# Two small reorderings in a Fourier-mixing and SwiGLU kernel: where the squares of a norm stand on ScalarE, and where the second filter product stands on VectorE

## The chip, the cores and the metric

The kernel runs on one core of one Trainium2 chip. Its time is the device time of one execution in microseconds (us). Before the change the median of three runs is 863.48 us (862.96 to 863.52). A profile of one execution is at hand as well; its own clock runs from the first to the last instruction.

A core has engines with a queue each: TensorE (PE in the profile, with its weight loads listed as PEld), VectorE (DVE), ScalarE (ACT), GpSimd (POOL) and SyncE (SP), which here only starts transfers. Each works through its own queue in order and waits there for semaphores of the others. TensorE writes its products into PSUM, which is cut into banks; VectorE and ScalarE read them out.

## The reference

The input x has 8 batches of 3008 positions with 256 features. Along the positions each feature is taken to its spectrum, multiplied by a complex filter, and brought back:

```python
X = np.fft.rfft(x, axis=1)
Y = X * (filt_r + 1j * filt_i)[None, :, :]
y = np.fft.irfft(Y, n=x.shape[1], axis=1)
```

The 24064 rows of y then go through a root-mean-square norm and a gated feed-forward of inner width 1536:

```python
xn = x / np.sqrt(np.mean(x * x, axis=-1, keepdims=True) + 1e-06) * rms_g
g = xn @ w_gate
out = (g * (1.0 / (1.0 + np.exp(-g))) * (xn @ w_val)) @ w_out
```

## The kernel before

The Fourier transform of length 3008 = 47 x 64 is done as products with small matrices, batch by batch, in four stages. The first stage (`a_unit`, line 201) is one product per unit, tile `psa`, 12 units per batch, read out to `t` and stored to memory. The middle stage (`b_unit`, line 236) takes four small products into one bank, tile `psb`, 16 units per batch. Its read-out is at the same time the product with the filter: two VectorE instructions, one with the real part (`s_part` with e = 0, line 231) and one with the imaginary part (e = 1, line 234). Both read the same bank, so the bank is free when the second is through. GpSimd adds the two (`add_unit`, line 268), and SyncE transposes the sum (`yt_load`, line 275). In batch 1 every fourth unit is a `b_soft` (line 247), which ScalarE copies out for GpSimd to work on. The third stage (`bi_unit`, line 280) multiplies back, tile `psi`, read out by ScalarE to `uu` (line 195). The last stage (`n_unit`, line 306) gives the rows of y, tile `psn`, read out by ScalarE. ScalarE then squares and sums these rows (`sq_unit`, line 322, one instruction for each 256 columns, so mostly two in a unit), GpSimd makes the scale from the sums (`stat_unit`, lines 330 and 332) and applies it (`xt_unit`), and SyncE transposes the scaled rows to `xn` (`tr_unit`).

The feed-forward is the bulk. It is cut into 576 slots: 8 batches, 6 groups of up to 512 rows, 12 blocks of 128 inner columns. In slot i, `gv` (line 533) makes four products of 512 columns on TensorE: two into `pg` (gate), two into `pv` (value). ScalarE then makes `sg` from `pg` (line 550), and VectorE multiplies `pv` by `sg` to `hh` (line 551). Two slots later `down` (line 554) multiplies `hh` with the output weights into `po`. Both `pg` and `pv` have two banks each, so the `pv` products of slot i+2 need `hh` of slot i to be through. The end of each group of 12 slots copies `po` out, half on ScalarE (line 568) and half on VectorE (line 569).

The Fourier stages of batch b+1 run between the feed-forward slots of earlier batches. They use two PSUM banks of one buffer each, called 0 (pool `psM`) and 3 (pool `psB`) in `bank` (line 189). A unit in bank 0 or 3 can begin its products only when the unit before it in that bank has been read out.

The order of the instructions is written out by hand: a planner (`fit`, line 734) gives every unit a slot from costs of ScalarE and VectorE and from when a bank is taken, and the list `plan[i]` holds the units of slot i. In that list the functions of `front` (line 720: squares, second filter product, add) stand ahead of the others, and so they also stand ahead in the engines' queues. The loop from line 837 emits, for every slot i, first `gv(i)`, then the units of `plan[i]`, then `down` of the item two slots back. So on VectorE a second filter product planned for slot i comes behind `hh` of slot i, and on ScalarE the order in a slot is `sg`, squares, read-outs. One exception stands in lines 832 to 834: where the next slot has an `a_unit` in bank 0 and this slot has a `bi_unit`, the squares go to the end of the list.

```python
            for fn, a in plan.pop(i, ()):
                fn(*a)
```

Of the kernel before, what the change touches and what calls it, by code (L numbers as in the profile page):

```python
# [101 lines left out]
def kernel(  # L102
# [430 lines left out]
    def gv(b, m, jt):  # L533
        n = nq(b, m)
        xn = st[b]["xn"][m]
        parts = ((0, 2), (2, 4)) if (b, m, jt) in SPLIT else ((0, n),)
        sg = hp.tile([P, 512], FP16, tag="sg", name="sg")
        hh = hhs[(6 * JT * b + JT * m + jt) % 4]
        made = []
        for q0, q1 in parts:  # L540
            w = (q1 - q0) * P
            pg = psG.tile([P, 512], FP32, tag="pg", name="pg")
            pv = psV.tile([P, 512], FP32, tag="pv", name="pv")
            for ps, wt in ((pg, wg), (pv, wv)):
                for dt_ in range(2):
                    nc.tensor.matmul(ps[:, 0:w], wt[:, dt_, ts(jt, P)], xn[:, q0:q1, dt_, :],  # L546
                                     start=(dt_ == 0), stop=(dt_ == 1))
            made.append((pg, pv, w, slice(q0 * P, q1 * P)))
        for pg, pv, w, c in made:
            nc.scalar.activation(out=sg[:, c], in_=pg[:, 0:w], func=AXT.Silu)  # L550
            nc.vector.tensor_tensor(out=hh[:, c], in0=pv[:, 0:w], in1=sg[:, c], op=ALU.mult)  # L551
        hh_of[(b, m, jt)] = hh

    def down(b, m, jt):
        hh = hh_of.pop((b, m, jt))
        if jt == 0:
            po_of[(b, m)] = [psO.tile([P, 2, D], FP32, tag="po%d" % i, name="po%d" % i)
                             for i in range(2)]
        po = po_of[(b, m)]

        n = nq(b, m)
        for s4 in range(n):
            nc.tensor.matmul(po[s4 // 2][:, s4 % 2, :], hh[:, ts(s4, P)], wo[:, jt, :],  # L563
                             start=(jt == 0 and s4 % 2 == 0),
                             stop=(jt == JT - 1 and (s4 % 2 == 1 or s4 == n - 1)))
        if jt == JT - 1:
            o3 = op.tile([P, 4, D], FP32, tag="o3", name="o3")
            nc.scalar.activation(out=o3[:, 0:2, :], in_=po[0], func=AXT.Copy)
            nc.vector.tensor_copy(out=o3[:, 2:n, :], in_=po[1][:, 0:n - 2, :])
            po_of[(b, m)] = o3  # L570

    def o_store(b, m):
        o3 = po_of.pop((b, m))
        w = 3 if m == 5 else 4
        if b == B - 1 and m == 5:
            row = lambda q, n: raw(out, b * N + 4 * m + q, [[N1 * D, N2], [H * D, 2], [1, n * D]])
            nc.sync.dma_start(row(0, 2), o3[:, 0:2, :].rearrange("p q d -> p (q d)"))
            nc.sync.dma_start(row(2, 1), o3[:, 2, :])
            nc.scalar.dma_start(raw(out, b * N + H - 1, [[N1 * D, N2], [-N * D, 2], [1, D]]), o3[:, 3, :])
            return  # L580
        nc.sync.dma_start(raw(out, b * N + 4 * m, [[N1 * D, N2], [H * D, 2], [1, w * D]]),
                          o3[:, 0:w, :].rearrange("p q d -> p (q d)"))
        if m == 5 and b % 2:
            nc.sync.dma_start(raw(out, b * N + H - 1, [[N1 * D, N2], [-N * D, 2], [1, D]]), o3[:, 3, :])
# [25 lines left out]
    with tc.manual_schedule():  # L610
# [108 lines left out]
        plan, late = {}, {}  # L719
# [109 lines left out]
            for m in range(6):  # L829
                norm_plan(b, m, (n_at + 8 * m, n_at + 8 * m + (4 if b > 1 else 2)), (2, 3, 7) if b > 1 else (2, 3, 6))  # L830

        for i, now in plan.items():
            if any(fn == a_unit and a[3] == 0 for fn, a in plan.get(i + 1, ())) and bi_unit in [fn for fn, _ in now]:
                now.sort(key=lambda u: u[0] == sq_unit)

        stores = {}
        for i in range(len(items) + 4):
            if i < len(items):
                gv(*items[i])
            for fn, a in plan.pop(i, ()):  # L840
                fn(*a)
            if 2 <= i < len(items) + 2:
                b, m, jt = items[i - 2]
                if jt == 1 and i > JT:
                    down(b, m, 0)
                if jt or i < JT:
                    down(b, m, jt)
                if items[i - 2][2] == JT - 1:
                    stores[i + 1] = items[i - 2][:2]
            for fn, a in late.pop(i, ()):  # L850
                fn(*a)
            if i in stores:
                o_store(*stores[i])
        assert not plan and not late


# [28 lines left out]
```

## Time and profile before

| | |
|---|---|
| median of the three runs | 863.48 us |
| profiled execution, first to last instruction (span) | 861.4 us |
| median less span | 2.1 us |
| TensorE busy | 852.4 us (99%) |
| VectorE busy | 557.2 us (65%) |
| ScalarE busy | 612.4 us (71%) |
| GpSimd busy | 297.8 us (35%) |
| granted TensorE clock | 0.999 of full speed |
| first feed-forward product | 43.4 us |
| last matmul | 856.3 us |

The profiled execution gives its span only; what lies around the span in a timed run is put at the 2.1 us between the two. The timeline lists instructions by engine in order of time: start, duration, engine, line, operation, written tile, read tiles, shapes; equal neighbours are drawn together with their number. A matmul's row begins where its product starts to flow; its successor starts while the row still lasts, so two rows of one engine overlap. The waits table lists, by engine, whom idle time before an instruction is put down to.

### The profile page before, as it was taken

The page shows a single profiled execution, that of the slowest core. Times are in us where ns is not written, and L with a number is a line of the kernel's source. Part 1 is how long each engine was busy: PE and PEld are TensorE (multiplying, and loading weights), DVE is VectorE, ACT ScalarE, POOL GpSimd, SP SyncE. Part 2 cuts the span into 40 slices and gives each one's busy share as a digit, 9 for nine tenths or more (in the row PEclk, how much of TensorE's full clock was granted, in tenths as well). Part 3 has the DMA queues.
Part 4 walks back from the last instruction along what each step waited for, and adds up shares of the span by engine and source line. Part 5 has one row for each costly group of instructions (what it writes and reads, how often), then busy time and mean ns, then how long its engine had stood idle before and what let it go on. Part 6 is the DMA issues. An engine that isn't in the chain of part 4 may idle for free.

```text
span 861.4 us, 17024 instructions
## 1 busy us (share of the span) xinstructions
PE 852.4 (99%) x6142; PEld 532.2 (62%) x6142; DVE 557.2 (65%) x926; ACT 612.4 (71%) x1339; POOL 297.8 (35%) x346
## 2 busy tenths in 40 slices
PE   8999999999999999999999999999999999999997
PEld 6755666566666666666666666666666666665664
DVE  5857655776666666666666676767666665555554
ACT  4986777787588756887577856888567765777443
POOL 5725742453144322534034430444123430132000
PEclk9999999999999999999999999999999999999999
DMA  9995778765975476656755548433564331521101
GB/s 283 270 204 124 150 164 168 139 130 121 197 137 129 121 150 111 151 107 147 139 127 113 132 98 180 108 87 101 131 127 93 97 70 42 124 54 49 62 25 50
DMA packets 198237, 107.98 MB, mean 125 GB/s; under 512 B 158566, under 2 KB 182520, under 8 KB 198152
## 3 DMA queue, kind: packets, MB, share of 16 engines
q1 hardware_dynamic: 189464, 85.52, 44.1%
q0 software_dynamic: 8544, 21.24, 12.7%
q8 instruction: 48, 0.79, 0.4%
q14 instruction: 37, 0.30, 0.1%
q10 hardware_dynamic: 144, 0.13, 0.0%
HBM read 45.78 MB, written 35.65 MB: 95 GB/s over the span
## 4 chain that ended last, share of the span: by engine, by line
PE 96%; DMA 1%; ACT 1%; DVE 1%; issue 0%; POOL 0%; POOLq 0%
PE po L563 28%; PE pg L546 28%; PE pv L546 28%; PE psb L241 3%; PE psi L285 3%; PE psn L314 2%; PE psa L206 2%; DMA fs<-in_filt_i_dram 1%; PE psy L418 1%; PE psf L389 1%; PE pst L367 0%; ACT sg L550 0%; POOL xc L186 0%; DVE s L231 0%; DVE hh L551 0%
## 5 line engine op out<-in xcount | busy, mean ns | idle before, releaser
L551 DVE TENSOR_TENSOR hh<-pv,sg 128x512 f16<-128x512 f32 (+2 forms) x578 | 391.5, 678 | 286.4 <-ACT sg L550 221.9
L550 ACT ACTIVATE sg<-pg 128x512 f16<-128x512 f32 (+2 forms) x578 | 337.4, 584 | 217.6 <-PE pg L546 213.4
L546 PE MATMUL pg<-xn,wg 128*128 128x512 f16 (+2 forms) x1156 | 338.1, 374 | 0.1
L546 PE MATMUL pv<-xn,wv 128*128 128x512 f16 (+2 forms) x1156 | 338.1, 374 | 0.0
L563 PE MATMUL po<-wo,hh 128*128 128x256 f16 x2256 | 332.7, 273 | 0.0
L563 PEld LDWEIGHTS <-hh 128*128 128x128 f16 x2256 | 213.4, 98 | 105.5 <-issue 0.6
L268 POOL TENSOR_TENSOR ss<-s,s 128x384 f16<-128x384 f16 x112 | 101.9, 911 | 273.2 <-DVE s L234 245.2
L546 PEld LDWEIGHTS <-wv 128*128 128x128 f16 x1156 | 112.9, 98 | 130.7
L546 PEld LDWEIGHTS <-wg 128*128 128x128 f16 x1156 | 111.4, 98 | 17.0 <-issue 0.3
L340 POOL TENSOR_TENSOR xt<-y,rho 128x1024 f16<-128x1024 f32 (+1 forms) x46 | 85.4, 1856 | 2.8
L322 ACT ACTIVATE junk<-y 128x256 f16<-128x256 f32 x180 | 74.3, 413 | 2.8
L231 DVE TENSOR_TENSOR s<-psb,ff 128x384 f16<-128x384 f32 x124 | 67.6, 547 | 0.7 <-ACT ff L195 0.6
L234 DVE TENSOR_TENSOR s<-psb,ff 128x384 f16<-128x384 f32 x124 | 67.6, 546 | 0.0
L195 ACT ACTIVATE uu<-psi 128x384 f16<-128x384 f32 (+1 forms) x127 | 61.6, 486 | 1.5 <-DMA out_dram<-o 0.5
L195 ACT ACTIVATE y<-psn 128x512 f32<-128x512 f32 (+1 forms) x95 | 55.7, 588 | 4.2
L285 PEld LDWEIGHTS <-yt 96*128 96x128 f16 x512 | 35.4, 97 | 26.7 <-issue 1.0
L332 POOL TENSOR_TENSOR rho<-u,mhalf 128x4 f32<-128x4 f32 (+1 forms) x46 | 46.5, 1010 | 3.8
L330 POOL TENSOR_SCALAR u<-ss 128x4 f32<-128x4 f32 (+1 forms) x46 | 8.9, 193 | 104.8 <-ACT junk L322 103.8
L195 ACT ACTIVATE t<-psa 128x512 f16<-128x512 f32 x70 | 41.4, 594 | 3.1 <-PE psa L206 1.7
L285 PE MATMUL psi<-wi,yt 96*128 96x96 f16 x512 | 42.9, 205 | 0.1
L241 PE MATMUL psb<-wb,t 96*128 96x96 f16 x480 | 40.1, 206 | 0.3 <-DVE s L234 0.2
L241 PEld LDWEIGHTS <-t 96*128 96x128 f16 x480 | 28.7, 97 | 12.8 <-DVE s L234 3.3
(101 smaller groups left out, 366.2 us busy)
## 6 DMA issues: line engine op xcount, KB each, us to landing
out_dram<-o SPq DMA_DIRECT2D x40, 512.0 KB, 3.6
xc<-in_x_dram POOLq DMA_DIRECT2D x31, 384.0 KB, 5.6
z_tmp<-t SPq DMA_DIRECT2D x28, 384.0 KB, 2.7
t<-z_tmp SPq DMA_DIRECT2D x28, 384.0 KB, 6.0
out_dram<-o SPq DMA_DIRECT2D x7, 384.0 KB, 2.7
fs<-in_filt_i_dram POOLq DMA_DIRECT2D x3, 512.0 KB, 10.8
fs<-in_filt_r_dram POOLq DMA_DIRECT2D x3, 512.0 KB, 11.2
ws<-in_moe_w_gate_dram POOLq DMA_DIRECT2D x3, 512.0 KB, 9.8
```

The lines of the kernel that those rows point to most:

```text
L195: nc.scalar.activation(out=out, in_=in_, func=AXT.Copy, **({} if scale is None else {"scale": scale}))
L231: eng.tensor_tensor(out=o, in0=ps, in1=f1, op=ALU.mult)
L234: eng.tensor_tensor(out=o, in0=ps[:, :, ::-1, :], in1=f2, op=ALU.mult)
L241: nc.tensor.matmul(ps[:, ts(k, KR)], st[b]["t2"][kk // KC][:, kk % KC, ds(dh * P, P)], wb[0:KR, kk, :], start=True, stop=True)
L268: nc.gpsimd.tensor_tensor(out=ss3[g % 3][:, :, dh, 0:KR], in0=s[0], in1=s[1], op=ALU.add)
L285: nc.tensor.matmul(ps[:, k, :], yt[0:KR, k, dh, :], wi[0:KR, 4 * g + k, :], start=True, stop=True)
L322: nc.scalar.activation(out=junk, in_=y[:, i, ts(u, D)], func=AXT.Square, accum_out=ss[:, 2 * i + u:2 * i + u + 1])
L340: nc.gpsimd.tensor_tensor(out=xt[:, 0:n, :], in0=y.rearrange("p a (u d) -> p (a u) d", u=2)[:, 0:n, :], in1=rho[:, 0:n].unsqueeze(2).to_br ...
L546: nc.tensor.matmul(ps[:, 0:w], wt[:, dt_, ts(jt, P)], xn[:, q0:q1, dt_, :], start=(dt_ == 0), stop=(dt_ == 1))
L550: nc.scalar.activation(out=sg[:, c], in_=pg[:, 0:w], func=AXT.Silu)
L551: nc.vector.tensor_tensor(out=hh[:, c], in0=pv[:, 0:w], in1=sg[:, c], op=ALU.mult)
L563: nc.tensor.matmul(po[s4 // 2][:, s4 % 2, :], hh[:, ts(s4, P)], wo[:, jt, :], start=(jt == 0 and s4 % 2 == 0), stop=(jt == JT - 1 and (s4 ...
```

## The change

A helper lists which PSUM banks the units of a slot use. With it two things are decided for every slot i, after the planner is done.

First, squares: where slot i has a read-out by ScalarE (a `bi_unit`, an `n_unit`, or an `a_unit` that ScalarE reads out) and slot i+1 uses bank 0, the squares go behind the other units of slot i. Before, this held only for a `bi_unit` ahead of an `a_unit` in bank 0.

Second, the second filter product: where slot i-1 has a `b_unit` whose bank slot i+1 uses, its second filter product is taken out of `plan[i]` and emitted at the start of slot i, ahead of `gv(i)`. On VectorE it so comes ahead of `hh(i)` instead of behind it.

```diff
-        for i, now in plan.items():
-            if any(fn == a_unit and a[3] == 0 for fn, a in plan.get(i + 1, ())) and bi_unit in [fn for fn, _ in now]:
+        def banks(i):
+            for fn, a in plan.get(i, ()):
+                if fn in (n_unit, bi_unit):
+                    yield 0
+                elif fn == a_unit:
+                    yield a[3]
+                elif fn == b_unit:
+                    yield a[2]
+                elif fn == b_soft:
+                    yield 3
+
+        early = {}
+        for i in sorted(plan):
+            now = plan[i]
+            after = set(banks(i + 1))
+            if any(fn in (bi_unit, n_unit) or (fn == a_unit and a[2] == "A") for fn, a in now) and 0 in after:
                 now.sort(key=lambda u: u[0] == sq_unit)
+            for fn, a in plan.get(i - 1, ()):
+                if fn == b_unit and a[2] in after:
+                    early[i] = [u for u in now if u == (s_part, (a[0], a[1], 1))]
+                    plan[i] = now = [u for u in now if u not in early[i]]
 
         stores = {}
         for i in range(len(items) + 4):
+            for fn, a in early.pop(i, ()):
+                fn(*a)
             if i < len(items):
                 gv(*items[i])
             for fn, a in plan.pop(i, ()):
...
-        assert not plan and not late
+        assert not plan and not late and not early
```

The planner's slots are the same before and after. Worked through the plan, the squares change place in slots 32, 34, 43, 45, 92 and 100, and the second filter product in 21 slots: 20, 22, 25, 27, 29, 31, 37, 39, 41 and 44 in batch 1, and 76, 78, 83, 85, 87, 90, 92, 97, 99, 104 and 106 in batch 2. From batch 3 on nothing moves. The queues of TensorE, GpSimd and SyncE keep their order throughout.

## The prediction

> **What bounds the kernel now.** The page first: TensorE is the chain that ended last.
>
> ```profile
> span 861.4 us, 17024 instructions
> PE 852.4 (99%) x6142; PEld 532.2 (62%) x6142; DVE 557.2 (65%) x926; ACT 612.4 (71%) x1339; POOL 297.8 (35%) x346
> PE 96%; DMA 1%; ACT 1%; DVE 1%; issue 0%; POOL 0%; POOLq 0%
> ```
>
> The reader sees that only time taken out of TensorE's queue can shorten the run; VectorE and ScalarE are idle a third of the span. Next the waits, from 60 to 210 us, where all moved instructions lie. TensorE's own:
>
> ```profile
> PEld L241 <- DVE s L234: 3.3, 7, 0.7
> PE psb L241 <- DVE s L234: 0.2, 1, 0.2
> ```
>
> The weight loads of the middle stage stood 3.3 us behind the second filter product, but a load that waits may still be hidden by running products, and idle time of TensorE itself is put at 0.2 us. From 210 us on the same view names no wait of TensorE at all. So I went to the timeline and read starts, not ends. In undisturbed slots a pair of 512-column products is followed 0.43 us later by the next product, a single one by 0.22, four 256-column ones by 0.43, four 96-column ones by 0.17. What a start comes later than that is a stall. Around 82 us:
>
> ```profile
> 81.43 0.55 DVE L231 TENSOR_TENSOR s<-psb,ff 128x384 f16<-128x384 f32 x1
> 81.89 0.68 DVE L551 TENSOR_TENSOR hh<-pv,sg 128x512 f16<-128x512 f32 x1
> 82.24 0.60 PE L546 MATMUL pv<-xn,wv 128*128 128x512 f16 x2
> 82.49 0.54 DVE L234 TENSOR_TENSOR s<-psb,ff 128x384 f16<-128x384 f32 x1
> 82.95 0.68 DVE L569 COPY o<-po 128x512 f32<-128x512 f32 x1
> 83.09 0.34 PE L241 MATMUL psb<-wb,t 96*128 96x96 f16 x4 [0.25 <-DVE s L234]
> 83.27 0.60 PE L546 MATMUL pg<-xn,wg 128*128 128x512 f16 x2
> 83.70 0.59 PE L546 MATMUL pv<-xn,wv 128*128 128x512 f16 x2
> 84.13 1.04 PE L563 MATMUL po<-wo,hh 128*128 128x256 f16 x8
> ```
>
> `pv` at 83.70 is followed by `po` at 84.13, as it should be. `pv` at 82.24 should be followed by `psb` at 82.67, but that started at 83.09, some 0.06 behind the end of the second filter product (82.49 + 0.54 = 83.03): a stall of 0.41. The filter product stood behind `hh`. The same on ScalarE at 93 us:
>
> ```profile
> 92.14 0.60 ACT L550 ACTIVATE sg<-pg 128x512 f16<-128x512 f32 x1 [0.21 <-PE pg L546]
> 92.37 0.34 PE L285 MATMUL psi<-wi,yt 96*128 96x96 f16 x4
> 92.63 0.41 ACT L322 ACTIVATE junk<-y 128x256 f16<-128x256 f32 x1
> 93.16 0.42 ACT L322 ACTIVATE junk<-y 128x256 f16<-128x256 f32 x1
> 93.58 0.47 ACT L195 ACTIVATE uu<-psi 128x384 f16<-128x384 f32 x1
> 93.58 0.60 PE L546 MATMUL pv<-xn,wv 128*128 128x512 f16 x2
> 93.95 0.59 ACT L550 ACTIVATE sg<-pg 128x512 f16<-128x512 f32 x1
> 94.10 0.38 PE L314 MATMUL psn<-t,tab 128*128 128x512 f16 x1
> ```
>
> `psi` is done by about 92.7, its read-out `uu` runs at 93.58 behind two squares, and `psn`, which wants the bank, starts at 94.10 instead of 94.01, 0.05 behind the end of `uu`.
>
> **The change part by part.** *Second filter product ahead of `hh`, 21 places.* No instruction is added. Its releaser, the first filter product, ends before `hh` in each of these slots, and the two run back to back with 0.46 us from start to start, so the bank comes free some 0.6 us earlier (slot 25: 81.89 + 0.54 = 82.43 instead of 83.03) or more where VectorE had idled before `hh`. With the 0.06 of release to start, slot 26's `psb` could begin at 82.49; it is due at 82.67, so its stall goes whole. Eleven of the 21 places have a stall in the next slot, each 0.05 to 0.15 us behind the end of that filter product: the product starts at 75.16 (0.09 us stalled), 78.25 (0.10), 83.09 (0.41), 89.21 (0.18), 113.48 (0.10), 156.06 (0.09), 159.15 (0.09), 166.84 (0.18), 169.91 (0.09), 188.85 (0.09) and 202.98 (0.09). Unrounded starts sum to 1.54 us. The ten other places have none; there nothing is won.
>
> *Squares behind the read-out, 6 places.* The read-out moves ahead by two squares, 93.58 - 92.63 = 0.95 us, less the time that `psi` is not done. Five stalls end 0.05 us behind such a read-out: `psn` at 94.10 (0.09), `psi` at 97.34 (0.26), `psn` at 111.80 (0.09), `psn` at 181.14 (0.26) and 193.80 (0.09). Unrounded 0.77 us. All are shorter than 0.95 less 0.11 (below), so all go. The sixth place, slot 45, has no stall behind it.
>
> *What it costs on VectorE.* `hh` must now wait for the second filter product: it starts at the earliest 2 x 0.46 us behind the start of the first. From the idle time before `hh` in the 21 slots (0 in three, at 81.89, 84.61 and 103.75; 0.11 to 0.32 in four; 0.37 or more in fourteen) that makes it 0.46 us late in three, at most 0.27 elsewhere, 2.0 us over all. Behind `hh` in VectorE's queue stand the next slot's `hh` or the copy of `po`; but these come no later than before, as the two instructions only change place. The one that waits for the late `hh` is `pv` two slots on: it started 1.13 us (slots 25 and 85) to 2.04 us behind the end of `hh`. The worst case is slot 25: 1.13 - 0.46 - 0.41 of stall gone leaves 0.26, against a release of 0.06. `po` in slot 27 wants its bank, which the copy `o` frees at 83.65 as before; its third product is due at 84.13 + 0.22 - 0.41 = 83.94: 0.29 to spare. So I cost the late `hh` at nothing; without that cover it would be up to 2.0 us once through.
>
> *What it costs on ScalarE.* The read-out may now wait for `psi` with the squares and the next `sg` behind it. Elsewhere `uu` starts 0.37 us behind `psi` (402.33 after 401.96), so at 92.74 instead of 92.63: 0.11 us idle, 0.7 over six places. It falls to the next `sg`, whose `pg` bank is wanted 1.51 us or more after it, and to `hh` behind it, whose `pv` bank has 1.22 us or more. Cost nothing.
>
> *GpSimd and the transfers.* Adds start up to 1 us earlier. In slots 34 and 45 the scale waits for the later squares, and adds queue behind it, by 0.5 us; transposed sums landed 4.0 to 7.0 us and `xn` 3.6 us or more before their first use. SyncE's queue has the same order. Nothing.
>
> *Sum.* 1.54 + 0.77 = 2.31 us off TensorE's queue, in a stretch (75 to 203 us) behind which it never waited, so the end moves as much: span 861.38 - 2.31 = 859.07. The median stands 2.1 us above the span; with that unchanged, 863.48 - 2.31 = 861.17, say 861.2 us (0.27% faster).
>
> *Against the idle rows.* By TensorE's idle time the two changes could win no more than 0.25 us (the one gap in brackets above), and the time would be 863.2. The Trainium skill, Perfetto Trace Analysis, section Tensor Engine Instruction (MATMUL, LD_WEIGHTS), says that a matmul's end in the profile is computed from its size, not observed, and so would have stalls hide inside "busy"; the starts above agree, and by it the sum stays with the starts.
>
> **The rivals.** *The stalls are none:* 99% busy is right, late starts are caught up in the products. Then 863.2. Against it: no product after a late start comes closer than the usual spacing (83.09, 83.27, 83.70, 84.13).
>
> *The wait moves.* VectorE has no idle time from 80.96 to 85.75, and its work there is not less; if half of the 2.31 us comes back at other banks, 862.3. For it: three `hh` late by 0.46. Against: 0.26 us is left at the tightest.
>
> *ScalarE held at its head:* the 0.11 us per place passes to TensorE through `sg`, 0.7 us, so 861.9. The same page of the Trainium skill, same section, calls ScalarE's queue strictly first in, first out, which speaks for such a loss; that the squares held up `uu` here agrees. Against it the 1.22 us above.
>
> *Slower:* the late `hh` reaches `pv` two slots on, at each of the 21 places, with the full 0.46 us: 9.7 us, less 2.3, so 870.9. It decides from where `hh` comes over 1.07 us late (1.13 less 0.06), and slower by over 0.2% needs 4.0 us of it. For it: VectorE's stretch without idle time. Against: idle time of 0.3 us or more before most `hh`.
>
> **How the numbers follow.** Forecast 0.72, no stalls 0.06, wait moves 0.08, ScalarE's head 0.06, slower 0.08. About 0.2% (1.73 us, so 861.75) is what a measurement of this kernel can tell from no change. Faster is the forecast alone, 0.72; the three middle cases give 0.20 within the bound; slower 0.08. The forecast's own range is 860.9 (a few small stalls more) to 861.7. To hold 8 in 10 the range takes in ScalarE's head and the moved wait, with 0.3 us for the spread of the runs (0.56): 860.8 to 862.6.
>
> **What would show it.** In the profile after: `psb` 0.43 us behind the `pv` pair at the eleven places, `psn` and `psi` likewise at five, the waits of weight loads on line 234 gone, from 210 us on the same times less 2.3 us. `hh` starts 0.46 us behind the second filter product at slots 25, 27, 39. Wrong it would be by a new gap before `pv` or `po` two slots after a moved product, or before a `pg` behind moved squares, or by stalls that stay where the bank is free.

## The result, and the profile after

The changed kernel takes 861.05 us in the median of 11 runs (860.79 to 862.05), the kernel before 863.23 us in 11 runs beside it (862.96 to 863.52). The ratio is 0.9976 with a 95% interval of 0.9968 to 0.9985: 2.18 us faster. 861.2 was predicted, in a range of 860.8 to 862.6.

The lines of the changed kernel's page that answer to those of before (of pages, waits and timelines only the rows that the text speaks of are shown here):

```profile
span 859.3 us, 17024 instructions
PE 849.6 (99%) x6142; PEld 532.8 (62%) x6142; DVE 557.2 (65%) x926; ACT 612.7 (71%) x1339; POOL 298.1 (35%) x346
PE 97%; DMA 1%; ACT 1%; DVE 0%; POOL 0%; issue 0%; POOLq 0%
```

The span is 2.1 us shorter, with nearly the same busy time on VectorE and ScalarE. TensorE shows 99% before and after: the share of busy time tells nothing of what changed. In the waits from 60 to 210 us the weight loads of the middle stage, 3.3 us behind the second filter product before, are down to these, the only two rows of TensorE that are left:

```profile
PEld L241 <- issue: 0.2, 1, 0.2
PEld L241 <- DVE s L234: 0.2, 1, 0.2
```

The second is the load at 82.54, and its product, in the timeline below, starts on time: a load can wait at no cost. The first is the load at 79.94 in slot 24, and there, as shown further down, a product does start late, though the view names no engine.

The timeline around slot 25, with the second filter product (line 234) now ahead of `hh`:

```profile
81.48 0.55 DVE L231 TENSOR_TENSOR s<-psb,ff 128x384 f16<-128x384 f32 x1
81.94 0.55 DVE L234 TENSOR_TENSOR s<-psb,ff 128x384 f16<-128x384 f32 x1
82.27 0.59 PE L546 MATMUL pv<-xn,wv 128*128 128x512 f16 x2
82.41 0.68 DVE L551 TENSOR_TENSOR hh<-pv,sg 128x512 f16<-128x512 f32 x1
82.70 0.34 PE L241 MATMUL psb<-wb,t 96*128 96x96 f16 x4
83.00 0.68 DVE L569 COPY o<-po 128x512 f32<-128x512 f32 x1
83.31 0.59 PE L546 MATMUL pv<-xn,wv 128*128 128x512 f16 x2
83.74 1.04 PE L563 MATMUL po<-wo,hh 128*128 128x256 f16 x8
```

`psb` starts 0.43 us behind the `pv` pair, where it was 0.85. `hh` starts 0.47 behind the second filter product, and ends at 83.09, 0.22 us before the `pv` of slot 27 at 83.31. The place on ScalarE, slot 32:

```profile
91.56 0.60 ACT L550 ACTIVATE sg<-pg 128x512 f16<-128x512 f32 x1 [0.21 <-PE pg L546]
91.80 0.34 PE L285 MATMUL psi<-wi,yt 96*128 96x96 f16 x4
92.17 0.49 ACT L195 ACTIVATE uu<-psi 128x384 f16<-128x384 f32 x1
92.55 0.41 ACT L322 ACTIVATE junk<-y 128x256 f16<-128x256 f32 x1
93.01 0.59 PE L546 MATMUL pv<-xn,wv 128*128 128x512 f16 x2
93.08 0.42 ACT L322 ACTIVATE junk<-y 128x256 f16<-128x256 f32 x1
93.44 0.38 PE L314 MATMUL psn<-t,tab 128*128 128x512 f16 x1
```

`uu` ends at 92.66, and `psn` follows its `pv` pair in 0.43 us. But a late start that was not there before has come, in slot 24:

```profile
78.47 0.41 ACT L322 ACTIVATE junk<-y 128x256 f16<-128x256 f32 x1
79.00 0.42 ACT L322 ACTIVATE junk<-y 128x256 f16<-128x256 f32 x1
79.41 0.47 ACT L257 ACTIVATE y<-psb 128x384 f32<-128x384 f32 x1
79.42 0.59 PE L546 MATMUL pv<-xn,wv 128*128 128x512 f16 x2
79.94 0.33 PE L241 MATMUL psb<-wb,t 96*128 96x96 f16 x4
```

`psb` is due at 79.85 and starts at 79.94, 0.06 behind the end of `y`, the copy of a `b_soft` in the same bank. That copy stands behind two squares, and the change moves squares only for other kinds of read-out. Before, TensorE had lost 0.19 us in two stalls ahead of this place, came later by that, and met a free bank.

All starts that come over 25 ns later than the usual spacing, from the first feed-forward product on, sum to 2.81 us before and 0.60 after: 2.21 us. From 60 to 210 us the gaps that no row of TensorE covers are only 0.47 us before (149.53 of 150 us busy) and none after (150.00), so most of the time won had stood inside rows that count as busy. The first feed-forward product started at 43.38 us before and at 43.53 after; in the profiles of this study that start lies between 43.29 and 43.68 whatever the edit.

### The profile page after: what moved, and what is told of

Same layout as the page of the kernel before. It is cut to its first block, busy times and chain, and to the rows that moved or that the text cites. A ratio compares the mean times of both kernels' runs of the same rounds, so it can differ in the third digit from the quotient of the medians.

```text
span 859.3 us, 17024 instructions
## 1 busy us (share of the span) xinstructions
PE 849.6 (99%) x6142; PEld 532.8 (62%) x6142; DVE 557.2 (65%) x926; ACT 612.7 (71%) x1339; POOL 298.1 (35%) x346
## 4 chain that ended last, share of the span: by engine, by line
PE 97%; DMA 1%; ACT 1%; DVE 0%; POOL 0%; issue 0%; POOLq 0%
PE po L563 29%; PE pv L546 28%; PE pg L546 28%; PE psb L241 3%; PE psi L285 3%; PE psn L314 2%; PE psa L206 2%; DMA fs<-in_filt_i_dram 1%; PE psy L418 1%; PE psf L389 1%; PE pst L367 0%; POOL xc L186 0%; DVE s L231 0%; ACT ff L195 0%; ACT L470 0%
```

## The experiments

The theory: products on TensorE start late where their bank is freed late, nothing catches such a start up, and the late starts add up to the difference in time. The rivals: the waits only move; the late `hh` costs; ScalarE is held by a read-out that waits. In this table "late starts" is that sum from the one trace of each kernel, and the last column is against the kernel before in the same comparison. The edits below are shown without the lines around them; they are made to the changed kernel, except where the text says otherwise.

| kernel | late starts, us | less those of before | median, us | median less before |
|---|---|---|---|---|
| before | 2.81 | | 863.22 to 863.26 | |
| changed | 0.60 | -2.21 | 861.05 | -2.18 |
| second filter product alone | 1.36 | -1.45 | 861.69 | -1.53 |
| squares alone | 2.25 | -0.56 | 862.67 | -0.55 |
| squares, and the filter product of slot 44 | 1.95 | -0.86 | 862.41 | -0.85 |
| filter product ahead everywhere | 0.59 | -2.22 | 861.12 | -2.10 |
| before, without the old exception | 5.61 | +2.80 | 865.93 | +2.71 |
| squares behind `b_soft` too | 0.53 | -2.28 | 860.93 | -2.33 |
| squares behind `b_soft`, and those of two more slots moved | 0.94 | -1.87 | 861.35 | -1.91 |

### One half alone: the second filter product

```diff
-            if any(fn in (bi_unit, n_unit) or (fn == a_unit and a[2] == "A") for fn, a in now) and 0 in after:
+            if any(fn == a_unit and a[3] == 0 for fn, a in plan.get(i + 1, ())) and bi_unit in [fn for fn, _ in now]:
```

> Only the second filter product goes ahead of hh (21 places); the squares stay as before. Theory (the stalls at single banks add up along TensorE's queue): the eleven stalls of 1.54 us go, the new one of 0.09 us in slot 24 appears as in the changed kernel, the five stalls behind squares (0.77 us) stay; 1.45 us faster than before, 0.17%. Rival (the wait moves: what is freed at one bank is lost at another unless squares move too): less than 0.8 us faster. Rival (the late hh costs, and the gain comes from the squares): no faster, or slower.

Measured: 861.69 us (861.46 to 862.09), ratio 0.9982 (0.9973 to 0.9991), 1.53 us faster. In the trace all eleven stalls are gone, the one of slot 24 is there (0.09), and the five behind squares stand at 0.09, 0.26, 0.09, 0.26 and 0.09 as before. This half works without the other. The rival by which it costs, and the one by which the freed time is lost elsewhere, fall.

### The other half alone: the squares

```diff
-                if fn == b_unit and a[2] in after:
+                if fn == b_unit and a[2] in ():
```

> Only the squares go behind the read-out (6 places); the second filter product stays behind hh. Theory: the five stalls of together 0.77 us go and the eleven of 1.54 us stay; 0.8 us faster than before, 0.09%, and with the other half alone the two sum to the whole change (2.2 us). Rival (ScalarE held at its head by a read-out that waits for psi): 0.1 us faster or nothing.

Measured: 862.67 us (862.57 to 863.0), ratio 0.9994 (0.9985 to 1.0003): 0.55 us faster where 0.8 was expected. The interval includes no change at all, though the runs of the kernel before lie higher, at 862.97 to 863.5; what follows rests on the trace. The five stalls are gone and ten of the eleven are unchanged to 5 ns. The eleventh, `psa` in slot 45, has grown from 0.10 to 0.31. The timeline of this kernel there:

```profile
109.49 0.60 ACT L550 ACTIVATE sg<-pg 128x512 f16<-128x512 f32 x1
109.72 0.34 PE L285 MATMUL psi<-wi,yt 96*128 96x96 f16 x4
110.10 0.49 ACT L195 ACTIVATE uu<-psi 128x384 f16<-128x384 f32 x1
111.43 0.58 ACT L550 ACTIVATE sg<-pg 128x512 f16<-128x512 f32 x1
112.04 0.69 DVE L551 TENSOR_TENSOR hh<-pv,sg 128x512 f16<-128x512 f32 x1 [0.76 <-ACT sg L550]
112.65 0.55 DVE L234 TENSOR_TENSOR s<-psb,ff 128x384 f16<-128x384 f32 x1
113.25 0.39 PE L206 MATMUL psa<-xc,tab 128*128 128x512 f16 x1
```

From `sg` to `sg` it is 111.43 - 109.49 = 1.94 us here; in the kernel before it was 1.82, as these two rows of its timeline show:

```profile
109.83 0.60 ACT L550 ACTIVATE sg<-pg 128x512 f16<-128x512 f32 x1
111.65 0.59 ACT L550 ACTIVATE sg<-pg 128x512 f16<-128x512 f32 x1
```

`uu` waits for `psi` 0.11 us, the squares and `sg` behind it start as much later, then `hh`, then the filter product behind `hh`, and `psa` waits for that. The other 0.09 of the growth is what TensorE had won in slot 44, and waits away here. So ScalarE held at its head did reach TensorE, at one place of six.

### The squares and one filter product

```diff
-                if fn == b_unit and a[2] in after:
+                if fn == b_unit and a[2] in after and i == 44:
```

> The squares behind the read-out, and the second filter product ahead of hh in slot 44 alone. With the squares alone the stall of psa in slot 45 grew from 0.10 to 0.31 us. Theory: the read-out in slot 43 holds ScalarE's queue for 0.11 us, which passes by sg and hh of slot 44 to the filter product behind hh, and 0.09 us won ahead of it is lost there too; with the filter product ahead of hh that stall goes whole: 0.77 + 0.10 = 0.87 us faster than before, 0.3 us faster than the squares alone. Rival (something else in slot 45 is late): as the squares alone, 0.55 us faster than before.

Measured: 862.41 us (862.23 to 862.99), ratio 0.9991 (0.9982 to 1.0): 0.85 us faster, and no late start in slot 45 in the trace. With the filter product ahead of `hh` the chain from `uu` to `psa` is cut at `hh`. So in the whole change the reordering on VectorE covers a cost of the reordering on ScalarE: by the traces the two halves alone win 1.45 and 0.56, 2.01 us together, and the whole change 2.21.

### The late `hh`, in all places

```diff
-                if fn == b_unit and a[2] in after:
+                if fn == b_unit:
```

> The changed kernel, with the second filter product ahead of hh in all 108 places instead of 21. In the 87 further places no bank is wanted in the next slot, so nothing is to be won there; hh comes later by 0 to 0.47 us, 7.4 us over all. Theory (the late hh is covered by the time until pv two slots on, 0.38 us or more after the shift): the same as the changed kernel within 0.1 us, 2.2 us faster than before. Rival (the late hh reaches TensorE): slower than the changed kernel by up to 7.4 us.

Measured: 861.12 us (860.93 to 861.23), ratio 0.9975 (0.9965 to 0.9985); the changed kernel ran at 861.05 and again at 861.07. `hh` starts later, counted from its own slot's first product, in 29 of the 87 further places, by up to 0.46 us and 7.3 us over all. The late starts on TensorE sum to 0.59 us as in the changed kernel. Of 7.3 us of lateness on VectorE nothing arrives. In these places at least 0.39 us was left between the end of `hh` and `pv` two slots on. TensorE's only wait from 60 us to the end is this one, the load of slot 24 again:

```profile
PEld L241 <- issue: 0.2, 1, 0.2
```

### More of the same cost: squares ahead in 14 more slots

This edit is made to the kernel before.

```diff
-        for i, now in plan.items():
-            if any(fn == a_unit and a[3] == 0 for fn, a in plan.get(i + 1, ())) and bi_unit in [fn for fn, _ in now]:
-                now.sort(key=lambda u: u[0] == sq_unit)
```

> The kernel before, with its old exception for squares taken out too: in 14 slots of batches 3 and 4 the squares stand ahead of the psi read-out where the next slot's psa wants the bank. Theory: the read-out ends 1.91 us after the start of that slot's sg, and psa starts 0.05 us later; against the starts of before this is a stall of 0.26 us in seven slots (136 to 172), 0.51 in two (210, 214) and 0.09 in five (202, 222 to 238): 3.25 us slower than before, 0.38%. Rival (such late starts are caught up and cost nothing at the end): no slower. Rival (the stall is only moved): less than 1.6 us slower.

Measured: 865.93 us (865.62 to 866.2), ratio 1.0031 (1.0019 to 1.0042): 2.71 us slower where 3.25 was expected. Slot 136 of this kernel and the `psa` behind it:

```profile
244.93 0.60 ACT L550 ACTIVATE sg<-pg 128x512 f16<-128x512 f32 x1 [0.88 <-PE pg L546]
245.42 0.41 ACT L322 ACTIVATE junk<-y 128x256 f16<-128x256 f32 x1
245.95 0.42 ACT L322 ACTIVATE junk<-y 128x256 f16<-128x256 f32 x1
246.20 0.59 PE L546 MATMUL pv<-xn,wv 128*128 128x512 f16 x2
246.37 0.47 ACT L195 ACTIVATE uu<-psi 128x384 f16<-128x384 f32 x1
246.89 0.38 PE L206 MATMUL psa<-xc,tab 128*128 128x512 f16 x1
```

`psa` is due at 246.63 and starts at 246.89: the stall of 0.26 that was worked out, and six of the seven slots have it to 2 ns, as five others have their 0.09. Slot 172 has none: one square stands ahead of its read-out there, not two. Slots 210 and 214 have 0.41 instead of 0.51: their `sg` has 384 columns, and the 1.91 us that were expected from its start to the end of the read-out hold for one of 512; here it is 1.81. Thirteen stalls, 2.78 us, make the 2.71.

### Two attempts at a version that beats both

```diff
+            if b_soft in [fn for fn, _ in now] and 3 in after:
+                now.sort(key=lambda u: u[0] == sq_unit)
```

> The changed kernel, with the squares of slot 23 behind the read-out of the b_soft there, whose bank slot 24 uses. Theory: the stall of 0.09 us that the change left in slot 24 goes. But the read-out waits 0.1 us for its product, sg and hh of slot 24 come that much later, and with them hh of slot 25, where pv two slots on had 0.23 us left; 0.23 - 0.11 - 0.09 leaves 0.03, under the 0.05 of a release, so up to 0.03 us may return there: 0.05 to 0.09 us faster than the changed kernel. Rival (0.03 us is no edge, more comes back): the same or slower than the changed kernel.

Measured: 860.93 us (860.78 to 861.13), ratio 0.9973 (0.9962 to 0.9984); beside it the changed kernel itself, whose expectation was

> The changed kernel once more, beside the next three on the same chip: 861.05 us, 2.2 us faster than before.

and which came to 861.07 us (860.86 to 861.13), 0.9974 (0.9964 to 0.9984). The stall in slot 24 is gone. A part came back, not at `pv` as expected but at `psb` in slot 26:

```profile
82.06 0.55 DVE L234 TENSOR_TENSOR s<-psb,ff 128x384 f16<-128x384 f32 x1
82.20 0.59 PE L546 MATMUL pv<-xn,wv 128*128 128x512 f16 x2
82.67 0.34 PE L241 MATMUL psb<-wb,t 96*128 96x96 f16 x4
```

`psb` starts 0.47 us behind the pair, 0.04 late. The lateness went there from `sg` of slot 24 (79.92, in the changed kernel 79.78) by its `hh` (80.53 and 80.40) and VectorE's queue to this filter product (82.06 and 81.94). By the traces 0.07 us is won; by the medians 0.14, with ranges that overlap. This is the fastest kernel of the study, by an amount that these runs don't resolve.

The second attempt adds to this:

```diff
+        for i in (352, 356):
+            sq = [u for u in plan[i] if u[0] == sq_unit]
+            plan[i] = [u for u in plan[i] if u[0] != sq_unit]
+            up_ = [u for u in plan[i + 1] if u[0] == a_unit]
+            plan[i + 1] = up_ + sq + [u for u in plan[i + 1] if u[0] != a_unit]
```

> As the run before, and the squares of slots 352 and 356 one slot later, behind the read-out of psa, for which psi of slots 354 and 358 were 0.05 us late each. Theory: 0.09 us more, so 0.14 to 0.18 us faster than the changed kernel, about 860.9 us. Rival: nothing is gained, since so small a stall is caught up.

Measured: 861.35 us (861.1 to 861.51), ratio 0.9977 (0.9968 to 0.9986): 0.42 us slower than the run before. The expectation fell. The two late starts of `psi` are gone, but the squares now stand ahead of the next `sg` and the read-out of `psi` (slot 354):

```profile
552.37 0.41 ACT L322 ACTIVATE junk<-y 128x256 f16<-128x256 f32 x1
552.65 0.34 PE L285 MATMUL psi<-wi,yt 96*128 96x96 f16 x4
552.90 0.42 ACT L322 ACTIVATE junk<-y 128x256 f16<-128x256 f32 x1
553.32 0.47 ACT L550 ACTIVATE sg<-pg 128x384 f16<-128x384 f32 x1
553.65 0.49 PE L546 MATMUL pv<-xn,wv 128*128 128x384 f16 x2
553.68 0.48 ACT L195 ACTIVATE uu<-psi 128x384 f16<-128x384 f32 x1
554.22 0.38 PE L314 MATMUL psn<-t,tab 128*128 128x512 f16 x1
```

`psn` is due 0.32 us behind its pair of 384 columns, at 553.97, and starts at 554.22, 0.05 behind the end of `uu`. Two stalls of 0.24 took the place of two of 0.05. Here the wait did move, and grew.

## Why the prediction was right

**The bound, read by starts.** The view that carried it was the spacing of starts in the timeline. The rival by TensorE's idle rows (863.2) is out, and so is every account in which a late start is caught up: over eight kernels the sum of late starts gives the median's difference to within 0.12 us. The Trainium skill, Perfetto Trace Analysis, section Tensor Engine Instruction (MATMUL, LD_WEIGHTS), says that a matmul's end is computed and not observed; the trace agrees in so far as the rows from 60 to 210 us left gaps of only 0.47 us before the change, where the starts were 2.35 us late.

**The second filter product, 1.54 us.** All eleven stalls went, as priced; 1.53 us alone in the medians, 1.45 in the trace after the new 0.09 of slot 24. That new stall was not foreseen: the working asked of each stall whether its bank comes free in time, but not what TensorE, earlier by 0.19 us, meets at the next bank that was only just free before. It is the rival "the wait moves", at about a thirteenth of its price (half of the 2.31 us). One of the waits of weight loads on line 234 that were to go is left, at 82.54, and costs nothing.

**The squares, 0.77 us.** The term holds in the whole change, where none of the five stalls is left. Alone it brings 0.55.

**The late `hh` at nothing.** Held. At the tightest of the 21 places, slot 25, 0.26 us was to be left and 0.22 was; with 7.3 us of lateness more the time stayed. (The copy of `po` ended at 83.63 before, not at 83.65; 0.31 us was to spare there, not 0.29.) "Slower" was far off: it wanted `hh` over 1.07 us late.

**The read-out that waits, at nothing.** Right in the sum, wrong in the cover that was named. The 0.11 us per place was right, and up to `pv` at least 1.02 us was left in the changed kernel, but the wait has a shorter way to TensorE: by `sg` and `hh` to the filter product behind `hh`. The squares alone lose 0.12 us by it in slot 45. In the change that way is closed because the filter product there goes ahead of `hh`. The strictly first-in-first-out ScalarE that the same section of the Trainium skill states showed as it says: what stood behind the waiting `uu` started as much later.

**The end.** 2.31 forecast, 2.18 measured: 0.09 is slot 24. From 210 us on no new late start came, so the end moved with the sum. That TensorE "never waited" there was read from the waits view and is not quite so: by starts, two `psi` are 0.05 us late each with the change and without it (554.97 and 559.70 before). That the time itself was met to 0.12 us (861.17 and 861.05) is in part luck: the median of three runs that it was counted from stood 0.25 above that of the eleven runs later, and this made up for the 0.13 that the gain was put too high. The 2.1 us between median and span have the same fault: each run's time stands some 1.8 us above its own span.

## What to carry to other kernels

Where one engine's queue is the chain that ends last, list its starts against its usual spacing, and find for each late one the instruction that frees its buffer: the sum of late starts is the most that freeing buffers earlier can win while that queue keeps its order, and here it told the gain to 0.13 us. An engine with idle time ahead of a dependent instruction can take in another one there for nothing, as long as the time until the next user of the delayed result is longer than the shift. Look after a won stall at the next just-free buffer, and after moved work at what it now stands in front of, in every queue: squares moved in two slots for the sake of two waits of 0.05 us made two of 0.24.

## What was not expected of the hardware

In the kernel before, the product that waited for a release by VectorE or ScalarE started 0.05 to 0.06 us after the end of that row, except in two places (slots 30 and 84) where it took 0.15 us: there TensorE's queue had a wait of its own ahead of the weight load (89.11 in slot 30), then the load (89.18), then the product (89.21). So the stalls there were 0.18 us, where the usual 0.06 would have made them 0.09. That the separate wait is the cause is not shown, but all of it vanished when the release came early.

The first feed-forward product starts between 43.29 and 43.68 us in ten profiles, at 43.53 and 43.63 in the two of the changed kernel; the edits all act later. That spread is as large as some of the differences that were asked for here; the late starts of a trace resolve 0.05 us where single spans do not.
